# Seven products of zeros ahead of the first attention scores of a three-block mixer kernel

## The chip, the cores and the metric

The kernel runs on one core of a Trainium2 chip, in one launch. The metric is the device time in microseconds (us) of that core, as a median over runs. Engines are called as the profile calls them: PE is TensorE's matrix product and PEld its weight load, DVE is VectorE, ACT is ScalarE, POOL is GpSimd, SP is SyncE, from whose queue all DMAs of this kernel are issued.

## The reference

Three blocks follow each other on two batches of 448 tokens and 768 channels: causal attention with 12 heads of 64, a mixer over tokens and channels, and a gated mixer. Only the first touches this change.

```python
def _attn_ref(q, k, v):                      # (2, 12, 448, 64) each
    scores = scale * np.matmul(q, k.transpose(0, 1, 3, 2))
    scores = np.where(mask, -1000000000.0, scores)
    scores = scores - np.max(scores, axis=-1, keepdims=True)
    attn = np.exp(scores)
    attn = attn / (np.sum(attn, axis=-1, keepdims=True) + 1e-09)
    return np.matmul(attn, v).astype(np.float32)

def _moe_ref(x, w_tok1, w_tok2, w_ch1, w_ch2):
    h = np.maximum(x.transpose(0, 2, 1) @ w_tok1, 0.0) @ w_tok2
    u = x + h.transpose(0, 2, 1)
    return (u + np.maximum(u @ w_ch1, 0.0) @ w_ch2).astype(np.float32)
```

The weights arrive as 64-bit floats; the kernel decodes them to 32 bits on chip (`decode`, L134 to L138) and splits them in two parts.

## The kernel before

**Attention.** The heads are taken two at a time: 12 pairs (b, n), six for each batch. For a pair, `prep_qk` loads k (L325) and the two halves of q (L327), and `load_v` loads v (L333). `probabilities` makes the scores of one half of the query rows of one head: PE multiplies q and k (L371, float32, moving widths of 64, 448, 128, 320 columns) into the tile `s_ps`, of which there are two buffers; DVE reads `s_ps`, adds the mask and takes the row extremes (L376, into `pe` and `mx`); ACT makes a bias of `mx` (L383) and the exponential (L385), then the 16-bit upper part (`hl`, L397); POOL, or DVE for a few, makes the lower part (L398); a transposing DMA on SP's queue turns both (`pT`, L401). A few of the 48 go through PE for the transposition instead (`t_ps`, L391). `values` multiplies `pT` with the two parts of v (`x_ps`, L424 to L426). The two parts of v, `vh` and `vl`, come from `prep_v`: a maximum of v on DVE (`am`, L340), a small product on PE that spreads it (`vm`, L342), `vh` on ACT (L347), `vl` on DVE (L348).

**Around it.** While attention runs, the token weights are decoded (ACT L134, DVE L137 and L138, POOL L145 and L108), the mixer over tokens runs for two pairs at a time (`a_ps`, `u_ps`), and the first products of the channel mixer (`r_ps`) are used to fill. From about 140 us on PE runs channel products and the gated block.

**What sets the order.** The program is written in one order, but a scheduler places the instructions of each engine: it keeps its own estimate of when operands are ready and gives a tile's instructions priorities (`high_priority` with negative offsets for the fill). Afterwards every engine works strictly through its own list, and so does SP's queue with the DMAs. An instruction that is added at the start can therefore change the lists behind it.

**The start.** The first pair's k and q are the first DMAs. Until they land PE has nothing to do. DVE sets q's unused quarters and parts of `vh` to zero meanwhile (L305 to L312), and POOL builds `ident` and `mask`.

Of the kernel before, what the change touches and what calls it, by code (L numbers as in the profile page):

```python
# [9 lines left out]
BF16 = mybir.dt.bfloat16  # L10
F16 = mybir.dt.float16
F32 = mybir.dt.float32
# [16 lines left out]
def mixer_kernel(  # L29
# [18 lines left out]
    nc = tc.nc  # L48
# [5 lines left out]
    P = 128  # L54
# [21 lines left out]
    const = ctx.enter_context(tc.tile_pool(name="const", bufs=1))  # L76
# [4 lines left out]
    rsum = sc.tile([P, B, NFF], F32, name="rsum")  # L81
    rs = ExitStack()
    rpool = rs.enter_context(tc.tile_pool(name="rpool", bufs=1))

    ident = const.tile([P, P], F32, name="ident")
    make_identity(nc, ident)
# [191 lines left out]
    with ExitStack() as at:  # L278
# [8 lines left out]
        ps_a = at.enter_context(tc.tile_pool(name="ps_a", bufs=1, space=PSUM))  # L287
        ps_u = at.enter_context(tc.tile_pool(name="ps_u", bufs=2, space=PSUM))
        ps_e = at.enter_context(tc.tile_pool(name="ps_e", bufs=2, space=PSUM))

        w1h = tokw.tile([P, NQ, T], F32R, name="w1h")
        w1l = tokw.tile([P, NQ, T], F32R, name="w1l")
# [666 lines left out]
```

## Time and profile before

| | |
|---|---|
| median of 3 runs | 405.92 us (405.43 to 406.95) |
| the profiled execution | 404.83 us, of which 403.0 us are the span from the first to the last instruction |
| PE busy | 387.5 us (96% of the span) |
| DVE, ACT, POOL busy | 296.7, 249.9, 188.8 us |
| the stretch of attention and token mixer | about 5 to 140 us |

A busy engine in the profile may be slow as well as full: a product's record lasts as long as the product takes at whatever clock it gets. The lists of the engines are given below as "order" listings; they tell what stands where, and nothing of times. A number behind a name there is the buffer's, and it differs between the two kernels by ten or so.

### The profile page before, as it was taken

What the parts mean: (1) busy time and instruction counts of PE and PEld (TensorE: products, weight loads), DVE (VectorE), ACT (ScalarE), POOL (GpSimd) and SP (SyncE); (2) the same over time, 40 slices, a digit from 0 to 9 for tenths busy, and PEclk for the clock granted to TensorE, in tenths of its full rate; (3) what the DMA queues carried; (4) which work ended last, traced back from release to release, by engine and by line L of the source; (5) the groups of instructions that cost most, each with busy time, mean ns of one, the idle gap of its engine ahead of it and who ended that gap; (6) DMA issues with size and microseconds to landing.
All of it is one profiled execution on the core that took longest, in us unless ns stands there. A gap on an engine that the chain in (4) does not pass through costs nothing.

```text
span 403.0 us, 7341 instructions
## 1 busy us (share of the span) xinstructions
PE 387.5 (96%) x2638; PEld 267.2 (66%) x2638; DVE 296.7 (74%) x709; ACT 249.9 (62%) x479; POOL 188.8 (47%) x195
## 2 busy tenths in 40 slices
PE   5988999989999999999999999999999999999996
PEld 3555777778887999999887555555554445555554
DVE  5988999767986825544367978778698998599742
ACT  3988778766977555755789793634275275655100
POOL 3865863684888464443352174254112158325200
PEclk9999999999999999999999999999999999999999
DMA  7999998999889835575640505545502322100122
GB/s 215 235 226 227 258 183 211 171 195 268 213 189 227 233 129 176 184 245 204 230 158 0 157 1 141 173 130 181 183 8 85 104 87 71 54 0 0 70 105 101
DMA packets 57524, 60.74 MB, mean 151 GB/s; under 512 B 43664, under 2 KB 49040, under 8 KB 57488
## 3 DMA queue, kind: packets, MB, share of 16 engines
q1 hardware_dynamic: 57488, 60.28, 57.0%
q8 instruction: 21, 0.34, 0.3%
q14 instruction: 15, 0.12, 0.1%
HBM read 47.29 MB, written 2.75 MB: 124 GB/s over the span
## 4 chain that ended last, share of the span: by engine, by line
PE 73%; DVE 12%; DMA 7%; ACT 3%; issue 2%; SPq 1%; POOL 1%; DVEq 0%; ACTq 0%; POOLq 0%
PE y_ps L214 7%; PE y_ps L212 7%; PE y_ps L213 7%; PE r_ps L212 6%; PE r_ps L214 6%; PE r_ps L213 6%; DMA vr<-in 3%; DVE pe L376 3%; PE o_ps L212 2%; PE o_ps L214 2%; PE ug_ps L213 2%; PE ug_ps L214 2%; PE o_ps L213 2%; PE ug_ps L212 2%; PE v_ps L213 2%; PE v_ps L212 2%
## 5 line engine op out<-in xcount | busy, mean ns | idle before, releaser
L371 PE MATMUL s_ps<-k,q 128*128 128x64 f32 (+3 forms) x216 | 54.8, 393 | 5.3 <-DMA q<-in 4.6
L108 POOL TENSOR_TENSOR wlo<-wm,whi 128x768 fp32r<-128x768 f32 x20 | 42.9, 2147 | 35.5 <-ACT whi L147 31.8
L212 PE MATMUL r_ps<-uh,whi 128*128 128x448 f32 x144 | 54.7, 380 | 0.0
L213 PE MATMUL r_ps<-ul,whi 128*128 128x448 f32 x144 | 52.9, 367 | 0.0
L214 PE MATMUL r_ps<-uh,wlo 128*128 128x448 f32 x144 | 52.9, 367 | 0.0
L398 POOL TENSOR_TENSOR hl<-pe,hl 128x512 f16<-128x512 f32 x34 | 42.2, 1245 | 18.3 <-ACT hl L397 14.9
L212 PE MATMUL y_ps<-r,w 128*128 128x448 f16 x144 | 50.6, 353 | 0.0
L213 PE MATMUL y_ps<-r,w 128*128 128x448 f16 x144 | 50.6, 352 | 0.0
L214 PE MATMUL y_ps<-r,w 128*128 128x448 f16 x144 | 50.4, 352 | 0.0
L134 ACT ACTIVATE wm<-wraw 128x768 f32<-128x768 f32 (+2 forms) x34 | 27.3, 804 | 34.5 <-DMA wraw<-in 27.3
L137 DVE TENSOR_SCALAR wm<-wm 128x768 int32<-128x768 int32 (+2 forms) x34 | 22.7, 668 | 29.6 <-ACT wm L134 29.6
L371 PEld LDWEIGHTS s_ps<-k,q 128*128 128x128 f32 x216 | 30.8, 200 | 12.8 <-DVE vh L310 4.6
L376 DVE CUSTOM_DVE_ANT_0 pe<-s_ps,mask 128x192 f32<-128x192 f32 (+3 forms) x84 | 34.5, 442 | 3.0 <-PE s_ps L371 2.8
L138 DVE SCALAR_TENSOR_TENSOR wm<-wraw,wm 128x768 int32<-128x768 int32 (+2 forms) x34 | 33.1, 973 | 0.7
L273 POOL TENSOR_TENSOR y<-yt,ul 128x448 f32<-128x448 f32 x10 | 13.2, 1322 | 42.7 <-DVE yt L271 42.7
L385 ACT ACTIVATE pe<-pe,bias 128x448 f32<-128x448 f32 (+3 forms) x67 | 32.2, 526 | 0.3
L424 PE MATMUL x_ps<-vh,pT 128*128 128x65 f16 (+1 forms) x240 | 25.6, 197 | 4.1 <-DMA pT<-hl 2.8
L212 PEld LDWEIGHTS r_ps<-uh,whi 128*128 128x128 f32 x144 | 27.1, 188 | 2.9 <-issue 0.4
L213 PEld LDWEIGHTS r_ps<-ul,whi 128*128 128x128 f32 x144 | 27.1, 188 | 2.9 <-issue 0.4
L424 PEld LDWEIGHTS <-pT 128*128 128x128 f16 (+1 forms) x240 | 21.2, 98 | 11.7 <-issue 5.3
L214 PEld LDWEIGHTS r_ps<-uh,wlo 128*128 128x128 f32 x144 | 27.0, 188 | 2.5
L206 POOL TENSOR_TENSOR w<-w2m,w 128x768 f16<-128x768 f32 x12 | 20.5, 1727 | 15.7 <-ACT w2m L205 12.8
(219 smaller groups left out, 1038.4 us busy)
## 6 DMA issues: line engine op xcount, KB each, us to landing
wraw<-in SPq DMA_DIRECT2D x36, 768.0 KB, 4.4
wraw<-in SPq DMA_DIRECT2D x14, 512.0 KB, 3.9
vr<-in SPq DMA_DIRECT2D x12, 320.0 KB, 4.3
k<-in SPq DMA_DIRECT2D x12, 224.0 KB, 3.7
q<-in SPq DMA_DIRECT2D x24, 112.0 KB, 3.8
out<-ob SPq DMA_DIRECT2D x11, 224.0 KB, 1.9
wraw<-in SPq DMA_DIRECT2D x3, 256.0 KB, 4.4
sgr<-in SPq DMA_DIRECT2D x3, 224.0 KB, 2.8
```

Source lines behind the costliest of these rows:

```text
L108: nc.gpsimd.tensor_sub(lo, src, f32(hi))
L134: nc.scalar.activation(m, words.bitcast(F32)[:, :, 1], AF.Prelu, scale=2.0 ** -112, alpha=-(2.0 ** 32))
L137: nc.vector.tensor_scalar(mi, mi, 3, None, ALU.logical_shift_left)
L138: nc.vector.scalar_tensor_tensor(mi, words[:, :, 0], 29, mi, ALU.logical_shift_right, ALU.bitwise_or)
L212: nc.tensor.matmul(ps, lh, rh, start=i == 0 and not begun, stop=False)
L213: nc.tensor.matmul(ps, lh, rl, start=False, stop=False)
L214: done.append(nc.tensor.matmul(ps, ll, rh, start=False, stop=ended and i == n - 1).ins)
L371: last_s[0] = nc.tensor.matmul(ps[:, o:o + m], qp[:, q0:q0 + P], k2[:, ks], start=True, stop=True).ins
L376: last_mx[0] = nc.vector.tensor_tensor_reduce(out=pe[:, cs], in0=ps[:, cs], in1=mask0 if i == 0 else mask[:, MASKS[i]], scale=-1.0 / math. ...
L385: nc.scalar.activation(pe[:, cs], pe[:, cs], AF.Exp, bias=bias[:, j:j + 1], scale=-1.0)
L398: ins = (nc.vector if lo_dve else nc.gpsimd).tensor_sub(hl[:, 1], pe, hl[:, 0]).ins
L424: nc.tensor.matmul(o, ph, vh[:, c, h, :D + 1], start=j == 0, stop=False)
```

## The change

A tile `warm` of 128x512 bfloat16 zeros is made by DVE, and seven products of it with itself, 128x512 each, are issued on PE into a PSUM tile that the token mixer uses later. Nothing reads them.

```diff
@@ -82,6 +82,9 @@
     rpool = rs.enter_context(tc.tile_pool(name="rpool", bufs=1))
 
+    warm = const.tile([P, 512], BF16, name="warm")
+    nc.vector.memset(warm, 0.0)
+
     ident = const.tile([P, P], F32, name="ident")
@@ -287,6 +290,10 @@
         ps_e = at.enter_context(tc.tile_pool(name="ps_e", bufs=2, space=PSUM))
+
+        pw = ps_a.tile([P, 512], F32, tag="a", name="warm_ps")
+        for _ in range(7):
+            nc.tensor.matmul(pw, warm[:, :P], warm, start=True, stop=True)
 
         w1h = tokw.tile([P, NQ, T], F32R, name="w1h")
```

Lines from L86 on move down by 3, and from L291 on by 7. The lists of all engines change with it. On PE, before: the nine products of the first pair's scores open the list.

```order
L371 MATMUL s_ps_207<-k2_182,q0_163 128x64
L371 MATMUL s_ps_207<-k2_182,q0_163 128x448
L371 MATMUL s_ps_229<-k2_182,q0_163 128x128
L371 MATMUL s_ps_229<-k2_182,q0_163 128x64
L371 MATMUL s_ps_229<-k2_182,q0_163 128x320
L371 MATMUL s_ps_295<-k2_182,q0_163 128x448
L371 MATMUL s_ps_306<-k2_182,q0_163 128x128
L371 MATMUL s_ps_306<-k2_182,q0_163 128x64
L371 MATMUL s_ps_306<-k2_182,q0_163 128x320
```

After, on PE, the end of the seven products and the scores behind them:

```order
L296 LDWEIGHTS warm_74
L296 MATMUL warm_ps_153<-warm_74 128x512
L378 MATMUL s_ps_217<-k2_192,q0_173 128x64
L378 MATMUL s_ps_217<-k2_192,q0_173 128x448
L378 MATMUL s_ps_239<-k2_192,q0_173 128x128
```

The first two rows stand seven times ahead of the scores, each product with a weight load of its own; the scores follow in the order they had. PE's two lists hold the same instructions from there on, in another order in places, up to the first `r_ps`, which starts at 79.8 us in the trace of before, and are nearly the same behind it.

On ACT, before, from the exponentials of the first `s_ps` on (`wraw` is a raw token weight):

```order
L385 ACTIVATE pe_208<-pe_208,bias_214 128x448
L397 CAST hl_219<-pe_208 128x512
L134 ACTIVATE wm_246<-wraw_195 128x256
L383 ACTIVATE bias_237<-mx_231 128x2
L385 ACTIVATE pe_230<-pe_230,bias_237 128x192
L385 ACTIVATE pe_230<-pe_230,bias_237 128x320
L383 ACTIVATE bias_298<-mx0_157 128x2
```

After, the same place on ACT:

```order
L392 ACTIVATE pe_218<-pe_218,bias_224 128x448
L390 ACTIVATE bias_247<-mx_241 128x2
L404 CAST hl_229<-pe_218 128x512
L392 ACTIVATE pe_240<-pe_240,bias_247 128x192
L392 ACTIVATE pe_240<-pe_240,bias_247 128x320
L137 ACTIVATE wm_256<-wraw_205 128x256
L390 ACTIVATE bias_308<-mx0_167 128x2
```

The second decode (`wraw_195`, now `wraw_205`) moved behind two exponentials, and the bias ahead of the cast. A third decode, `wm_380`, which stood 11 rows further down, moved some 40 rows down, with its DVE and POOL instructions; its DMA moved 20 rows down on SP.

On DVE, before, from the second `vl` on (each 128x1 `mx` row belongs to the row above it; `am_370` is the maximum of the third pair's v, `vr_368`):

```order
L348 SCALAR_TENSOR_TENSOR vl1_181<-vr_197,sv_327,vh1_177 128x640
L376 ISA pe_659,mx_660<-s_ps_658,mask_87 128x192
L376 ISA mx_660 128x1
L376 ISA pe_659,mx_660<-s_ps_658,mask_87 128x320
L376 ISA mx_660 128x1
L376 ISA pe0_155,mx0_157<-s_ps_691,mask_87 128x448
L376 ISA mx0_157 128x1
L340 TENSOR_REDUCE am_370<-vr_368 128x1
```

After, the same place on DVE:

```order
L355 SCALAR_TENSOR_TENSOR vl1_191<-vr_207,sv_337,vh1_187 128x640
L347 TENSOR_REDUCE am_380<-vr_378 128x1
L383 ISA pe_669,mx_670<-s_ps_668,mask_89 128x192
L383 ISA mx_670 128x1
L383 ISA pe_669,mx_670<-s_ps_668,mask_89 128x320
L383 ISA mx_670 128x1
L383 ISA pe0_165,mx0_167<-s_ps_701,mask_89 128x448
L383 ISA mx0_167 128x1
```

The maximum of v moved ahead of three reads of scores. On SP the load of that v, which stood behind four transposing DMAs, stands behind three.

## Rows read from the trace of the kernel before

**Rows 1.** Stretches: busy us and instructions of each engine, granted clock, DMA share, GB/s.
```profile
core 0: us, PE busy (x) PEld busy (x) DVE busy (x) ACT busy (x) POOL busy (x), PEclk, DMA share, GB/s
4.60:11.40 6.80, 6.80 (x21) 4.46 (x21) 3.91 (x19) 4.45 (x10) 2.25 (x3) 1.00 0.96 291
11.40:24.00 12.60, 10.33 (x97) 6.47 (x97) 11.16 (x41) 12.50 (x32) 9.66 (x10) 1.00 1.12 219
24.00:80.00 56.00, 52.38 (x589) 40.84 (x588) 50.10 (x161) 43.83 (x102) 34.43 (x45) 1.00 1.01 214
80.00:140.00 60.00, 58.06 (x550) 50.13 (x549) 47.22 (x110) 45.79 (x99) 44.04 (x48) 1.00 0.99 219
140.00:390.00 250.00, 250.00 (x1332) 159.28 (x1329) 177.59 (x364) 143.29 (x238) 96.32 (x77) 1.00 0.36 116
```

**Rows 2.** Groups by shape, PE from 4.5 to 10 us: busy us, mean ns.
```profile
L371 PE MATMUL s_ps<-k,q 128*128 128x448 f32 x4 | 3.5, 981 | 0.0
...
L371 PE MATMUL s_ps<-k,q 128*128 128x64 f32 x4 | 1.2, 401 | 4.6 <-DMA q<-in 4.6
```

**Rows 3.** The same, PE from 28 to 40 us.
```profile
L371 PE MATMUL s_ps<-k,q 128*128 128x448 f32 x8 | 3.9, 575 | 0.0
...
L371 PE MATMUL s_ps<-k,q 128*128 128x64 f32 x10 | 1.7, 257 | 0.0
```

**Rows 4.** Timeline, PE: start, us, instructions; two records make a product.
```profile
4.60 6.79 PE L371 MATMUL s_ps<-k,q 128*128 128x64 f32 x18 [4.60 <-DMA q<-in]
...
31.32 2.13 PE L371 MATMUL s_ps<-k,q 128*128 128x64 f32 x10
...
259.98 0.35 PE L214 MATMUL y_ps<-r,w 128*128 128x448 f16 x1
260.17 0.35 PE L212 MATMUL y_ps<-r,w 128*128 128x448 f16 x1
```

**Rows 5.** Instructions that write or read `vm` (L342): min, median, max ns.
```profile
L342 PEld LDWEIGHTS <-am x4: 96/97/98, 11.0 to 28.9; 128*128 128x128 bf16 x4
```

**Rows 6.** Timeline, DVE.
```profile
0.87 0.43 DVE L305 MEMSET q<- 64x448 f32 x1 [0.87 <-PEq L944]
1.44 0.43 DVE L306 MEMSET q<- 64x448 f32 x1
...
7.03 0.22 DVE L376 CUSTOM_DVE_ANT_0 pe<-s_ps,mask 128x64 f32<-128x64 f32 x1 [1.98 <-PE s_ps L371]
...
20.93 0.36 DVE L376 CUSTOM_DVE_ANT_0 pe<-s_ps,mask 128x192 f32<-128x192 f32 x1
...
21.62 0.62 DVE L376 CUSTOM_DVE_ANT_0 pe<-s_ps,mask 128x448 f32<-128x448 f32 x1
...
23.66 0.69 DVE L340 TENSOR_REDUCE am<-vr 128x1 bf16<-128x512 f32 x1 [1.41 <-DMA vr<-in]
```

**Rows 7.** Timeline, ACT.
```profile
7.84 0.20 ACT L383 ACTIVATE bias<-mx 128x2 f32<-128x2 f32 x1 [0.28 <-DVE mx L376]
8.08 0.91 ACT L385 ACTIVATE pe<-pe,bias 128x64 f32<-128x64 f32 x2
9.01 0.62 ACT L397 CAST hl<-pe 128x512 f16<-128x512 f32 x1
10.36 0.44 ACT L134 ACTIVATE wm<-wraw 128x256 f32<-128x256 f32 x1 [0.73 <-DMA wraw<-in]
...
14.43 0.43 ACT L134 ACTIVATE wm<-wraw 128x256 f32<-128x256 f32 x1
```

**Rows 8.** Timeline, SP's queue: start and us of the issue.
```profile
13.79 2.75 SPq L401 DMA_TRANSPOSE pT<-hl  x2
...
17.93 1.40 SPq L401 DMA_TRANSPOSE pT<-hl  x1
19.43 0.53 SPq L333 DMA_DIRECT2D vr<-in  x1
```

**Rows 9.** Waits of PE from 11 to 80 us, then of DVE from 5 to 80 us: total, times, longest.
```profile
PE x_ps L424 <- DMA pT<-hl: 2.8, 3, 1.4
...
DVE am L340 <- DMA vr<-in: 4.2, 3, 1.8
```

## The prediction

> **What bounds the kernel now.** I read the stretches first. From 140 to 390 us PE is busy in 250.00 of 250.00 us [rows 1]: whatever time PE wins or loses before it gets there moves the end by the same amount, since no wait is left in it that could swallow a gain. So the change is worth what it does to the moment at which PE is through with attention. Ahead of 140 us the reader should look at how much room there is: PE is busy throughout 4.60 to 11.40 us (6.80 of 6.80), then it idles 2.27 us up to 24 us, 3.62 us from there to 80 us and 1.94 us up to 140 us [rows 1]. In 11.40 to 24 us it is not PE but ACT that is full, 12.50 of 12.60 us, with DVE at 11.16; from 24 to 80 us PE (52.38 of 56.00) and DVE (50.10) stand close together [rows 1].
>
> Second, the shapes. The granted clock reads 1.00 in every stretch, but the durations of the first products contradict it: the same 448-column product takes 981 ns up to 10 us and 575 ns from 28 us on, the 64-column one 401 against 257 ns [rows 2, 3]. The difference for 448 columns is 406 ns, for 64 columns 144 ns, so it is 262 ns for 384 columns more; what grows with the columns takes 1.51 ns a column (580/384) at first and 0.83 ns (318/384) later, close to a factor of two. I take it that the first products ran at the lower level (1.2 GHz), after an idle PE, and the later ones at the upper one (2.4 GHz), and that the clock column simply holds no record of the start. Third, the lists of the engines, since the change moves instructions; fourth, what ACT, DVE and SP do there [rows 6 to 8].
>
> **The seven products and their tile.** DVE's first instruction starts at 0.87 us, and a memset of 448 words takes 0.43 us, with 0.57 us from one start to the next [rows 6]. The new one, 256 words of the same width, takes about 0.25 us, so PE can begin at about 1.3 us. No bfloat16 product of 512 columns is in the trace; the nearest is the 16-bit one of 448 columns, which follows its predecessor by 0.19 us at the upper level [rows 4]. That gives 0.22 us for 512 columns, or 0.43 us at the lower level: seven take 1.5 to 3.0 us. A weight load of 128 columns in bfloat16 takes 97 ns [rows 5]; if none of the seven hides behind a product, add 0.7 us. They end between 2.8 and 5.0 us, most likely at 4.3 us, at the lower level with the loads hidden. The first scores start at 4.60 us, because q lands then [rows 4]; PE's idle start is the cover, and the cost is nothing, at worst 0.4 us. On DVE the memset pushes the zeros of q and what follows by 0.25 to 0.57 us; the 1.98 us that DVE idles until 7.03 us hide it [rows 6]. Without that cover it would cost just that much. q's DMAs don't queue behind it.
>
> **What the clock gives.** The nine score products of the first pair have 1984 columns and take 6.79 us in 18 records; five of a later pair, 1024 columns, take 2.13 us at the upper level [rows 4]. At that rate 1984 columns take 4.13 us, so 2.66 us is the most that the clock can return on PE. How long the lower level lasted follows from the same two: what it cost, 2.66 us, is 0.45 of its length at the ratio of 1.51 to 0.83 ns a column, and half of it at a ratio of two, so 5.3 to 5.9 us; I take 5.7 us, since everything up to 10 us is long [rows 2] and PE began at 4.60 us. If the seven products start the same delay at 1.3 us, the rise comes at about 7.0 us, 2.4 us into the scores: the loss shrinks to 2.4/5.7 of it, and 1.5 us are returned. Bounds: 0 (the zeros or the small gap behind them do not carry over) and 2.66 us (full from the first score). I take 1.5 us, as the row is the only delay that this trace shows.
>
> The Trainium skill, "TensorE: Matmul & The Clock Gate", Part 1, speaks against taking one delay over: it says that the moment of the rise is not tied to the kernel's start, and that the same kernel gets a different number of slow products from run to run. One profiled execution can't show that. By it the sum would lie anywhere between the two bounds just named, and it would be no truer at 1.5 us than at 2 us.
>
> **How much of that arrives.** From 11.40 to 24 us ACT is full, so PE's 1.5 us arrive only as far as ACT gets ahead. ACT loses two waits there in the first 11 us: 0.28 us for the first `mx` and 0.73 us for a raw token weight [rows 7]. The new list has that decode two exponentials later, when its weight has landed (it landed at 10.36 us), and the next bias ahead of the cast; so the 0.73 us become a wait for the second product's `mx`, which is shorter the faster that product ran. Of the 1.01 us I count half, 0.5 us, because the first product, which DVE begins to read at 7.03 us [rows 6], would still run at the lower level by the delay taken above, and only the second one gains. The third decode, 0.43 us on ACT at 14.43 us [rows 7], leaves the full stretch and is paid back after 24 us, where ACT has 12 us of room (43.83 of 56.00) [rows 1]. Sum on ACT at 24 us: 0.9 us, with bounds of 0.43 and 1.44 us. ACT's 0.9 us are less than PE's 1.5, so they count.
>
> **What the new order gives or takes.** Behind that, the lists differ up to about the first `r_ps`. PE does the same work, so only its idle time can change: 2.27 + 3.62 = 5.89 us from 11.40 to 80 us [rows 1], of which 2.8 us are waits for transposed probabilities [rows 9]. I see no row that says that the new order has more or less of it, and put it at nothing; the bounds are the rivals below. The sum is -0.9 us. Against the profiled execution, 404.83 us (403.0 us of span), that makes 403.9 us; the median of the runs stands 1.09 us above that execution, so the forecast is 405.0 us. A difference of 0.5%, 2 us, is about what a measurement of this kernel can tell from no change; this lies inside it.
>
> **Rival: slower, DVE is blocked on v.** DVE works in order, and its waits for v's loads already cost 4.2 us in three places [rows 9]. In the largest early one, before, DVE had read three scores (20.93 to 22.24 us) and then waited 1.41 us [rows 6]. Now the maximum of v stands ahead of those reads. The load was issued at 19.43 us and landed 4.2 us later, at about 23.6 us. In the new list three, not four, transposing DMAs stand ahead of it, so it can go out from 16.5 us (13.79 + 2.75) [rows 8], or, if the buffer of v comes free late, as before: it lands between 20.7 and 23.6 us. Then the maximum (0.69 us) and the three reads (1.31 us) end between 22.7 and 25.6 us, where the reads ended at 22.24 us: exponentials, transposes and values of that pair come 0.5 to 3.4 us later, though v's own chain comes earlier. It decides from a landing at about 21.2 us on, where the delay passes the 0.9 us won. With the worst of it, 3.4 - 0.9 = 2.5 us slower: 408.4 us; in the middle, 2.0 - 0.9 = 1.1 us slower: 407.0 us. Against it: one transposing DMA less ahead of the load, and a decode less on DVE ahead of the maximum.
>
> **Rival: faster, everything arrives.** The clock is up with the first score and ACT and DVE take the scores as they come: -2.66 us, 403.3 us. If the new order also removes the 2.8 us of PE's waits for transposes [rows 9], 400.5 us. For it: DVE waits 1.98 us for the first score and would take it earlier [rows 6]. Against it: ACT, full to 24 us.
>
> **Rival: the clock doesn't rise earlier.** Then only the order acts: the third decode's 0.43 us leave ACT's full stretch, and the time is 405.5 us, in the same class as the forecast.
>
> **How the numbers follow.** The forecast (gain of some 0.4 to 1.5 us, the order neutral) 0.38; no earlier rise 0.12; faster with clock and order together 0.31; slower by DVE's block 0.19, half of it past 2 us, though other waits of this kind in the moved part (the lists differ for 60 us) can take its place, so I leave nearly all of it on the slower side. That is faster 0.31, same 0.51, slower 0.18. The range leaves out the outer half of the faster rival and of the slower one: from 401.9 us (half way from 403.3 to 400.5) to 407.7 us (half way from 407.0 to 408.4).
>
> **What would show it.** In the trace after: seven products from about 1.3 to 4.3 us and the first score still at about 4.6 us (right on cover); the 448-column product of the first score shorter than 981 ns, the first one of 575 ns before 7.5 us (right on the clock); the nine products done by 9.7 us instead of 11.4; ACT without the 0.73 us wait; the first `r_ps` about 0.9 us before 79.8 us, and the same gain at the end. It is wrong if the first score starts after 5 us, if its products still take 981 ns up to 10 us, if DVE's waits for v grow past 4.2 us, or if PE's idle time from 11.4 to 80 us differs from 5.9 us by more than 2 us: then the order, not the clock, made the result.

## The result, and the profile after

The changed kernel takes 410.18 us (408.00 to 412.31, median of 8 runs), the kernel before 405.89 us in the same comparison: a ratio of 1.0101, with a 95% interval of 1.0069 to 1.0132. It is slower by 4.3 us, where 405.0 us were forecast and 407.7 us was the end of the range. The profiled execution of the changed kernel is its quickest, 408.0 us, of which 406.2 us are the span: 3.2 us more than before.

Stretches of the kernel after, with the columns of [rows 1]:

```profile
core 0: us, PE busy (x) PEld busy (x) DVE busy (x) ACT busy (x) POOL busy (x), PEclk, DMA share, GB/s
4.60:11.40 6.80, 6.32 (x20) 3.98 (x21) 4.12 (x22) 4.47 (x10) 0.78 (x1) 1.00 0.92 287
11.40:24.00 12.60, 11.34 (x103) 7.32 (x104) 11.56 (x46) 11.54 (x30) 10.14 (x11) 1.00 0.96 196
24.00:80.00 56.00, 49.40 (x565) 38.22 (x563) 47.04 (x150) 43.89 (x100) 35.86 (x48) 1.00 0.90 202
80.00:140.00 60.00, 57.61 (x527) 49.34 (x524) 46.62 (x112) 46.06 (x100) 42.54 (x44) 1.00 0.99 225
140.00:390.00 250.00, 250.00 (x1356) 160.45 (x1355) 180.10 (x368) 144.83 (x242) 97.25 (x79) 1.00 0.35 117
```

Against [rows 1], PE's idle time is 0.48 us more up to 11.4 us, 1.0 us less from there to 24 us (1.26 for 2.27), 3.0 us more up to 80 us (6.60 for 3.62) and 0.45 us more up to 140 us: 2.9 of the 3.2 us in all. From 140 to 390 us both run without a gap. So the start did gain, by half a microsecond, and the stretch from 24 to 80 us lost six times as much.

The start, on PE (start, us, instructions):

```profile
1.17 3.17 PE L296 MATMUL warm_ps<-warm 128*128 128x512 bf16 x7 [1.17 <-DVE warm L86]
4.77 4.88 PE L378 MATMUL s_ps<-k,q 128*128 128x64 f32 x12 [0.44 <-DMA q<-in]
9.87 1.22 PE L378 MATMUL s_ps<-k,q 128*128 128x128 f32 x6 [0.21 <-DVE mx L383]
10.93 0.22 PE L349 MATMUL vm<-ident_b,am 128*128 128x128 bf16 x1
```

The same scores by shape, PE from 4.5 to 10 us (busy us, mean ns), to be held against [rows 2]:

```profile
L378 PE MATMUL s_ps<-k,q 128*128 128x448 f32 x4 | 2.7, 774 | 0.0
...
L378 PE MATMUL s_ps<-k,q 128*128 128x64 f32 x4 | 1.2, 400 | 0.4 <-DMA q<-in 0.4
```

The products end at 4.34 us, ahead of the scores; the 64-column product is as slow as before (400 for 401 ns), the 448-column one quicker on average (774 for 981 ns). That fits a clock that rises in the middle: the first clock record of the trace, which is the rise, stands at 8.7 us, before at 10.4 us.

And waits of PE from 11 to 80 us and of DVE from 5 to 80 us (total, times, longest), to be held against [rows 9]:

```profile
PE x_ps L431 <- DMA pT<-hl: 3.8, 6, 1.0
PE s_ps L378 <- DVE mx L383: 1.6, 5, 0.4
PE u_ps L498 <- DVE al L488: 1.2, 1, 1.2
```

```profile
DVE pe L383 <- PE s_ps L378: 5.7, 6, 1.8
DVE am L347 <- DMA vr<-in: 4.4, 5, 2.1
```

PE's waits are more and shorter than before: six for transposed probabilities instead of three. None of them is the 3 us by itself. The first `r_ps`, which stood at 79.81 us, comes late, in spite of the gain at the start:

```profile
82.03 0.45 PE L215 MATMUL r_ps<-uh,whi 128*128 128x448 f32 x1
```

### The profile page after: what moved, and what is told of

Its sections match the earlier page's. It is cut to its first block, busy times and chain, and to the rows that moved or that the text cites. A ratio compares the mean times of both kernels' runs of the same rounds, so it can differ in the third digit from the quotient of the medians.

```text
span 406.2 us, 7349 instructions
## 1 busy us (share of the span) xinstructions
PE 390.9 (96%) x2645; PEld 267.9 (66%) x2645; DVE 296.9 (73%) x710; ACT 250.8 (62%) x479; POOL 188.7 (46%) x195
## 4 chain that ended last, share of the span: by engine, by line
PE 73%; DVE 10%; DMA 9%; issue 3%; ACT 2%; SPq 1%; POOL 1%; DVEq 0%; ACTq 0%; POOLq 0%
PE y_ps L215 7%; PE y_ps L216 7%; PE y_ps L217 7%; PE r_ps L215 7%; PE r_ps L216 7%; PE r_ps L217 7%; DMA vr<-in 6%; PE s_ps L378 3%; DVE pe L383 3%; PE o_ps L217 2%; PE o_ps L215 2%; PE o_ps L216 2%; PE ug_ps L216 2%; PE ug_ps L217 2%; PE ug_ps L215 2%
## 5 line engine op out<-in xcount | busy, mean ns | idle before, releaser
L378 PE MATMUL s_ps<-k,q 128*128 128x64 f32 (+3 forms) x216 | 53.8, 389 | 3.3 <-DVE mx L383 2.2
L140 DVE TENSOR_SCALAR wm<-wm 128x768 int32<-128x768 int32 (+2 forms) x34 | 21.7, 638 | 33.3 <-ACT wm L137 33.3
L141 DVE SCALAR_TENSOR_TENSOR wm<-wraw,wm 128x768 int32<-128x768 int32 (+2 forms) x34 | 35.0, 1028 | 0.6
```

The lines of the kernel that those rows point to most:

```text
L140: nc.vector.tensor_scalar(mi, mi, 3, None, ALU.logical_shift_left)
L141: nc.vector.scalar_tensor_tensor(mi, words[:, :, 0], 29, mi, ALU.logical_shift_right, ALU.bitwise_or)
L378: last_s[0] = nc.tensor.matmul(ps[:, o:o + m], qp[:, q0:q0 + P], k2[:, ks], start=True, stop=True).ins
```

## Experiment 1: products and lists apart

The change does two things: it adds products, and it moves the lists. To take them apart, the lists were written down from both kernels and put back with ordering edges between an engine's neighbours, edges that carry no semaphore:

```diff
         mixer_kernel(tc, *args)
+        in_this_order(nc, tc)
```

`w7_old` has the seven products with the lists of before, `w0_new` no products with the lists of after. `w5_old` has five products (with five, the scheduler leaves the lists alone), `w12_old` twelve with the lists of before.

```diff
-        for _ in range(7):
+        for _ in range(12):
```

> The seven products of zeros, with every engine's list in the order of the kernel before (pinned by issue-order edges). Theory A, the moved lists cost the 4.3 us: with the old lists the kernel is back at 405.9 us or a little below it, 404.4 to 406.2 us, since the clock rises some 1.7 us earlier (8.7 us in the trace after, 10.4 us in the trace before). Theory B, the products themselves cost it (they start PE early, the clock falls again or rises at another time, and later stretches run at the lower level): 409 to 411 us, and a mean granted clock below 1.0 in most executions. A mixture (3 us from the lists, 1 to 2 us from the clock) would show as 406.5 to 408 us.

> No products and no tile of zeros; every engine's list in the order of the kernel after. Theory A: the loss stays, 408.5 to 411 us. Theory B: 405 to 406.5 us. If the products give a gain of their own, this one is slower than the kernel after by that gain, 0.5 to 1.5 us.

> Five products in place of seven, nothing pinned: the scheduler then leaves every list as before. Theory A: 404.4 to 406.2 us. Theory B, if the loss is in the products: about five sevenths of it, 408 to 409.5 us. The five end at about 3.3 us, 1.3 us before the first scores; if the early start counts for the clock all the same, it rises before 10.4 us.

> Twelve products with the old lists: 12 x 0.43 us from 1.2 us on end at 6.3 us at the lower level, so the first score starts 1.7 us late, but with no idle PE in front of it. Theory A with a gain from the clock: the clock rises before the first or second score, PE makes up what it started late, 405 to 406.5 us. If PE's early time is not what bounds the kernel there but the chain of DVE and ACT behind the first score, the late start shows in full: 407 to 407.6 us.

Measured, as ratios to the kernel before (406.59 us) with 95% intervals; a ratio is not simply the quotient of the two medians:

| kernel | median us | ratio |
|---|---|---|
| `w7_old` | 405.46 | 0.9976 (0.9954 to 0.9998) |
| `w0_new` | 410.18 | 1.0086 (1.0059 to 1.0113) |
| `w5_old` | 406.33 | 1.0002 (0.9985 to 1.0019) |
| `w12_old` | 407.28 | 1.0023 (0.9997 to 1.0048) |

Without a single product, the moved lists alone take the time of the changed kernel, within the intervals (1.0086 against 1.0101). With the lists held, none of the three numbers of products moves the ratio by more than 0.25%; twelve land where the late start was expected to show (407 to 407.6 us), but the interval still includes no change. The ordering edges are not what costs, since `w7_old` has them as well. The loss is the lists'.

The shapes tell how far the products did their work. The 448-column scores from 4.5 to 10 us, in `w7_old`:

```profile
L378 PE MATMUL s_ps<-k,q 128*128 128x448 f32 x4 | 2.0, 579 | 0.0
```

and in `w0_new`, which has none:

```profile
L371 PE MATMUL s_ps<-k,q 128*128 128x448 f32 x4 | 3.0, 836 | 0.0
```

In `w7_old` all of them run at the upper level (575 ns in [rows 3]); in the changed kernel, with the same seven products, part of them. In `w0_new` without products they are nearly as quick as after (836 against 774 ns), in `wnewold` of experiment 3, also without products, just as quick (773 ns), and before they are slow throughout (981 ns). So the moment of the rise differs between executions by as much as seven products move it. In the profiled execution of `w7_old` PE's products got most of the 2.66 us of the prediction's bound: nine take 4.5 us where before they took 6.79. But PE then waits for DVE, and the nine end only 0.7 us earlier, at 10.7 us:

```profile
4.62 3.23 PE L378 MATMUL s_ps<-k,q 128*128 128x64 f32 x12 [0.37 <-DVE vh L317]
9.50 1.22 PE L378 MATMUL s_ps<-k,q 128*128 128x128 f32 x6 [1.66 <-DVE mx L383]
```

The stretches of the same execution:

```profile
4.60:11.40 6.80, 5.12 (x22) 3.17 (x23) 4.67 (x23) 4.43 (x10) 2.25 (x3) 0.96 0.98 282
11.40:24.00 12.60, 10.01 (x78) 5.86 (x77) 10.62 (x40) 11.97 (x32) 9.51 (x10) 0.89 1.18 216
```

PE idles 1.68 and 2.59 us here where before it idled 0 and 2.27, and the granted clock, 0.89 in the second stretch, has gone back to the lower level for part of it. This execution is the slowest of the twelve of `w7_old` (408.03 us); nine of them have a mean clock of 1.0 and take 404.85 to 407.01 us. So it shows one way in which a gain at the start can be lost, not what the median run does.

## Experiment 2: one place in the lists?

The trace of after has one place that looks like the loss. DVE, from 47 to 53 us:

```profile
47.33 0.68 DVE L141 SCALAR_TENSOR_TENSOR wm<-wraw,wm 128x512 int32<-128x512 int32 x1
49.24 0.36 DVE L383 CUSTOM_DVE_ANT_0 pe<-s_ps,mask 128x192 f32<-128x192 f32 x1 [1.23 <-PE s_ps L378]
...
52.15 0.69 DVE L347 TENSOR_REDUCE am<-vr 128x1 bf16<-128x512 f32 x1 [2.13 <-DMA vr<-in]
```

SP's queue around the load that DVE waits for:

```profile
40.83 0.33 SPq L123 DMA_DIRECT2D wraw<-in  x1
41.27 1.25 SPq L408 DMA_TRANSPOSE pT<-hl  x1
42.63 0.96 SPq L123 DMA_DIRECT2D wraw<-in  x1
43.70 4.10 SPq L408 DMA_TRANSPOSE pT<-hl  x2
47.86 0.57 SPq L340 DMA_DIRECT2D vr<-in  x1
```

The load goes out at 47.86 us behind five others, though v's buffer was free from 39.6 us on, when the last reader (`vl`, 1.77 us from 37.85 us) ended; before, its counterpart went out at 37.20 us. DVE stands 2.13 us. A second candidate is the third slab of the first weight matrix, whose decoding has moved from 14 us to the 36 to 41 us in which DVE is full. `v_first` has the lists of after with the load alone moved up:

```diff
 L327 DMA q_164<-in 64x448 x2
+L333 DMA vr<-in 128x640
 L120 DMA wraw<-in 128x512
 L401 DMA_TRANSPOSE pT<-hl 128x8x128
 L120 DMA wraw<-in 128x512
-L401 DMA_TRANSPOSE pT<-hl 128x8x128 x2
-L333 DMA vr<-in 128x640
-L401 DMA_TRANSPOSE pT<-hl 128x8x128
+L401 DMA_TRANSPOSE pT<-hl 128x8x128 x3
```

`w_early` has the slab where it was, on SP, ACT, DVE and POOL; on ACT:

```diff
 L385 ACTIVATE pe<-pe,bias 128x320
+L134 ACTIVATE wm<-wraw 128x256
 L383 ACTIVATE bias<-mx 128x2
...
 L393 ACTIVATE pT<-t_ps 128x512
-L134 ACTIVATE wm<-wraw 128x256
 L347 ACTIVATE vh_177<-vr,sv 128x10x64
```

`vw` has both edits, and `c_oldnew` the lists of before up to about 37 us and those of after behind that.

```diff
-PE, DVE, ACT, POOL, SP: entries of after from 0 on
+PE, DVE, ACT, POOL, SP: entries of before up to 257, 85, 59, 41, 34, of after from there on
```

> No products, every list as in the changed kernel but one entry: the load of v that VectorE waits for at 50 us stands six places earlier in SP's list, right behind the two q loads that precede it there by 8 us. Theory V (that late load is the loss of 50 to 53 us): VectorE's wait of 2.1 us goes, and 1.5 to 2.1 us of the 3.5 us that the new lists cost come back, 408.1 to 408.7 us, ratio 1.004 to 1.005. Rival (VectorE is ahead of TensorE there, its wait on scores 1.2 us just before says so, and the wait only changes its name): under 0.5 us, 409.7 us or more.

> No products, every list as in the changed kernel but for the third slab of the first weight matrix: its load, ScalarE's conversion, VectorE's two decoding steps and GpSimd's two splits stand where the kernel before has them, at 13 to 16 us, not at 31 to 41 us. Theory W (the decoding, 0.4 + 1.2 us on VectorE at 36 to 41 us, holds up the masks that TensorE waits for there): 1.2 to 1.6 us come back, 408.6 to 409.0 us, ratio 1.005 to 1.006. Theory V: the loss sits later, so at most 0.5 us, 409.7 us or more.

> Both edits of the two kernels beside it at once, no products. If two separate places make the loss, their gains add: 2.7 to 3.5 us come back, 406.7 to 407.5 us, ratio 1.000 to 1.002. If one place hides the other, it is no better than the better of the two, 408.1 us or more.

> No products; the lists of the kernel before up to about 37 us (the first 257 of TensorE's entries, 85 of VectorE's, 59 of ScalarE's, 41 of GpSimd's, 34 of SP's hold the same instructions in both versions), those of the changed kernel from there on, the late load of v included. Theory V (the loss is made behind the cut): 409 to 410 us, ratio 1.006 to 1.009. Theory W (it is made ahead of the cut, by the slab's late decoding): 406.3 to 407.3 us, ratio 0.999 to 1.002.

| kernel | median us (before: 406.39) | ratio |
|---|---|---|
| `v_first` | 408.15 | 1.0058 (1.0029 to 1.0088) |
| `w_early` | 409.54 | 1.0081 (1.0051 to 1.0110) |
| `vw` | 409.40 | 1.0089 (1.0056 to 1.0121) |
| `c_oldnew` | 408.40 | 1.0055 (1.0028 to 1.0082) |

DVE's wait for v is gone in `v_first`, and the wait for scores ahead of it has stayed:

```profile
49.05 0.36 DVE L376 CUSTOM_DVE_ANT_0 pe<-s_ps,mask 128x192 f32<-128x192 f32 x1 [1.27 <-PE s_ps L371]
...
49.74 0.68 DVE L340 TENSOR_REDUCE am<-vr 128x1 bf16<-128x512 f32 x1
```

The median of `v_first` is 2 us lower than that of `w0_new`, its ratio lower by 0.0028 with intervals that overlap: the load may be worth 1 to 2 us here, and not all of the loss. (The execution profiled is the quickest of its twelve, 405.98 us.) The slab is worth nothing that shows. The two edits together are no better than the lists they started from: `vw` differs from `w_early` by the same load, and there moving it returned nothing (1.0089 for 1.0081). `c_oldnew` lies between what both theories gave: by the medians about half of the loss comes with the later lists.

## Experiment 3: the halves again, and the load in three settings

`on_v` is `c_oldnew` with the load moved up; `wnewold` has the lists of after first (with the slab as before, since the later lists need it) and those of before from the same cut on; `w7_v` is the changed kernel with the load moved up, products and all.

```diff
 L327 DMA q_163<-in 64x448 x2
+L333 DMA vr<-in 128x640
 L325 DMA k_1110<-in 128x448
...
-L333 DMA vr<-in 128x640
```

```diff
-PE, DVE, ACT, POOL, SP: entries of after from 0 on
+PE, DVE, ACT, POOL, SP: entries of after up to 257, 85, 59, 41, 34, of before from there on
```

> No products; the lists of the kernel before up to about 37 us and those of the changed kernel behind it, as in the run that took 408.4 us (ratio 1.0055), but with the late load of v moved six to nine places up in SP's list, to where the kernel before issues it. Theory V (that one load makes most of the loss behind 37 us): 1.5 to 2.0 us come back, 406.4 to 406.9 us, ratio 1.000 to 1.002. Rival S (the loss is many small waits of TensorE, none of which is this load's): under 0.5 us, 407.9 us or more, ratio 1.004 or more.

> No products; the other half: the changed kernel's lists up to about 37 us, but with the third slab of the first weight matrix where the kernel before has it (the lists behind need it there), and the lists of the kernel before from 37 us on. If the loss lies behind the cut alone: 406.2 to 406.9 us, ratio 0.999 to 1.002. If the lists ahead of the cut also cost (the kernels that carry them had their clock recorded at the half level about twice as often as those that don't): 407.2 to 408.4 us, ratio 1.002 to 1.005.

> The changed kernel itself, seven products and its lists, with that one load of v six places earlier in SP's list. Theory V: 1.5 to 2 us of the changed kernel's 410.2 come back, and the products, worth 0.9 us with the lists held, may show: 407.3 to 408.7 us, ratio 1.002 to 1.006. Rival S: 409.5 us or more, ratio 1.007 or more.

| kernel | median us (before: 405.95) | ratio |
|---|---|---|
| `on_v` | 408.17 | 1.0049 (1.0014 to 1.0083) |
| `wnewold` | 412.13 | 1.0145 (1.0101 to 1.0188) |
| `w7_v` | 408.39 | 1.0067 (1.0032 to 1.0102) |

In `on_v` the edit did what it should and returned nothing (408.40 to 408.17). Waits of DVE from 37 to 80 us, in `c_oldnew`:

```profile
DVE am L340 <- DMA vr<-in: 3.6, 3, 2.8
DVE sv L344 <- PE vm L342: 2.2, 1, 2.2
DVE rd L452 <- PE x_ps L426: 1.5, 1, 1.5
```

and in `on_v`:

```profile
DVE sv L344 <- PE vm L342: 2.6, 1, 2.6
DVE rd L452 <- PE x_ps L426: 1.9, 2, 1.5
...
DVE am L340 <- DMA vr<-in: 1.2, 2, 0.7
```

The wait for v shrank by 2.4 us, but the two waits for PE grew by 0.8 us, and PE's idle time from 24 to 80 us stayed (5.78 and 5.59 us). That fits a DVE that was ahead of PE there, as far as one execution of each can tell. In `w7_v` the same edit returned 1.8 us by the medians (410.18 to 408.39; in the ratios 0.0034, with intervals that overlap), as it had returned 2.0 in `v_first`. So in the lists of after that load may be a third to a half of the loss, and with other lists ahead of it (`on_v`, `vw`) it returns nothing that shows. And `wnewold` was a surprise: the earlier lists of after, with the slab moved back, followed by the later ones of before have a higher ratio than either whole. A half of a list is good or bad together with the other half, so "which place is it" has no single answer in these runs. The theory of one place had fallen as the whole answer, and what was left to try was that the lists of before are good as a whole.

## Experiment 4: other lists from the same scheduler

If the lists of after are bad in some way of their own, other lists should fall on either side of before. If those of before are unusually good, all others should be slower. Six, eight, nine and ten products each make the scheduler write different lists, which differ from those of before and of after in hundreds of rows. The edit is the count alone:

```diff
-        for _ in range(7):
+        for _ in range(6):
```

> Six products, and the planner's own lists for that, which differ from those of the kernel before and from those of seven products. Theory N (one place in the lists of seven products is bad): the lists of six have another such place or none, so the time may fall on either side of before, 404.5 to 408 us, ratio 0.997 to 1.005. Theory L (the lists of the kernel before are an unusually good draw, and any other that the planner makes costs about 1%): 408.5 to 411.5 us, ratio 1.006 to 1.014.

> Eight products with the planner's own lists, again different from all others. Theory L: 408.5 to 411.5 us, ratio 1.006 to 1.014. Theory N: on either side of before, 404.5 to 408 us, ratio 0.997 to 1.005.

> Nine products with the planner's own lists, again different. Theory L: 408.5 to 411.5 us, ratio 1.006 to 1.014. Theory N: on either side of before, 404.5 to 408 us, ratio 0.997 to 1.005.

> Ten products with the planner's own lists, again different. Theory L: 408.5 to 411.5 us, ratio 1.006 to 1.014. Theory N: on either side of before, 404.5 to 408 us, ratio 0.997 to 1.005.

| products, own lists | median us (before: 406.19) | ratio |
|---|---|---|
| 6 | 413.27 | 1.0161 (1.0110 to 1.0211) |
| 8 | 412.76 | 1.0152 (1.0104 to 1.0199) |
| 9 | 411.97 | 1.0130 (1.0088 to 1.0171) |
| 10 | 421.01 | 1.0362 (1.0321 to 1.0403) |

(The planner in the expectations is the scheduler.) All are slower, by more than was expected, and one by 15 us; of the five sets of lists that were tried with their products, those of seven cost least. Where each loses differs. PE's idle time in the profile of eight products sits from 80 to 140 us (7.6 us), in that of ten also behind 140 us (6.1 us), where before there is none:

```profile
80.00:140.00 60.00, 52.42 (x490) 44.17 (x490) 43.06 (x113) 42.37 (x91) 41.52 (x44) 1.00 0.87 213
```

```profile
140.00:200.00 60.00, 53.88 (x321) 48.19 (x322) 27.60 (x43) 30.35 (x60) 22.82 (x19) 0.91 0.52 154
```

The first fence is of eight products, the second of ten. So in this kernel other lists from the same scheduler cost 1.0 to 3.6%, and those of eight and of ten do not lose in the same place. (The products themselves vary too, but with the lists held five, seven and twelve were worth no more than 0.25%.) What the lists of before have that all these lack is not shown. Nor are the five independent draws. In their traces all five put the load of v ahead of the fourth transposing DMA, and all five hold the third slab's load back: it goes out at 9.39 us before, at 15.52 us with ten products and at 28.9 us or later with the others. The slab alone returned nothing in `w_early`, but a cause that the early rows of all five share is not excluded, and the ratio of `wnewold` would fit one. Lists that differ from before for a reason other than these products were not tried.

## Why the prediction was wrong

**Cover, right.** The products run from 1.17 to 4.34 us (about 1.3 to 4.3 forecast), and the first score starts at 4.77 us for 4.60, released by q's DMA.

**Clock, right in kind, not in its worth.** The rise came earlier, but at 8.7 us and not at 7.0; the nine scores were done at about 11.1 us rather than 9.7, and ACT's wait of 0.73 us became one of 0.60 us for `mx`. ACT's busy time from 11.4 to 24 us fell from 12.50 to 11.54 us, about the 0.9 us of the sum, of which the third decode that moved away is 0.43. With the lists held, seven products gave a ratio of 0.9976, about 1 us. That is close to the 0.9 us of the sum, but the agreement proves little: with the lists of after they gave nothing (410.18 us with and without), and five and twelve gave nothing either. So the term is between 0 and 1 us, and these runs don't tell more. The Trainium skill, "TensorE: Matmul & The Clock Gate", Part 1, says that the moment of the rise is not tied to the kernel's start and that one kernel gets a different number of slow products from run to run. The shapes agree, over different kernels with the same nine scores: the 448-column mean is 773 to 981 ns in the eight without products, and 774, 579 and 758 ns in the three with seven. In those three the products start alike, at 1.17 us, and the rise is recorded at 8.7, 4.0 and 6.3 us. One profiled execution of before could not carry a delay of 5.7 us.

**Order, the step that failed.** "I see no row that says that the new order has more or less of it, and put it at nothing." It cost 3.6 us in `w0_new` (410.18 against 406.59 us), four times the term that the sum rested on. The lack of a row was read as zero, with chances on both sides; yet the lists differ for 60 us on five engines, and each of the five other sets that the scheduler wrote here lost, 0.9 to 3.6%. The prediction's own signs came close to naming it: PE's idle time from 11.4 to 80 us went from 5.89 to 7.86 us, and the first `r_ps` came 2.2 us late where 0.9 us early was forecast. The same step held that PE does the same work, so that only its idle time can change; that left out a clock that falls back later (the mean granted clock is below 0.999 in 12 of the 14 runs with the lists of after).

**Rival "slower", right in direction, not in its place.** DVE's wait for the third v, on which it was priced, was harmless: the load went out at 17.32 us and DVE waited 0.43 us for it, where before it waited 1.41. DVE's waits for v's loads as a whole are 4.4 us, as they were 4.2: by the letter a sign of being wrong, but 0.2 us explain nothing. That another wait of this kind can take its place, as the prediction added, holds in part: it is the load of experiment 2.

```profile
20.54 0.69 DVE L347 TENSOR_REDUCE am<-vr 128x1 bf16<-128x512 f32 x1 [0.43 <-DMA vr<-in]
```

**Open.** How the 4.3 us divide is not settled to the last. In runs with a mean granted clock of 0.999 or more the lists of after take 407.7 and 408.0 us (two runs, of `w0_new` and of the changed kernel), the kernel before 405.8 us (mean of 49 runs): so about 2 us are lost at full clock. The other 12 of these 14 runs have a lower mean clock, against 47 of 96 runs of before, and take 408.2 to 412.3 us. At an equal clock, 0.995 to 0.996, eight of them average 410.0 us and 40 runs of before 406.9 us, 3.1 us apart. So the larger part of the loss is there at an equal clock, and the lower clock adds the smaller part. Why these lists lose is open beyond the waits shown. `w7_old` has the lowest median, but its interval (0.9954 to 0.9998) all but reaches no change.

## What to carry to other kernels

An edit that a scheduler sees changes more than its own instructions: compare the lists first, and don't price a changed list at zero. Here five new sets out of five were worse; whether other kernels share that is not shown. Hold the lists and measure the edit alone; here that turned 1% slower into no loss. And before a wait in a trace is called the loss, ask who would be late next: moving the load that ends a 2 us wait of DVE returned 1 to 2 us by the medians with one set of lists and nothing with another, where DVE then waited longer for PE.

## What the hardware showed that was not expected

TensorE's clock need not stay up once it has risen. In the profile of `c_oldnew`, in the middle of attention, the granted clock falls to the lower level of 1.2 GHz for part of two stretches. Stretches of 3 us, with the columns of [rows 1]:

```profile
48.00:51.00 3.00, 2.42 (x23) 1.68 (x22) 1.91 (x6) 3.00 (x8) 1.69 (x2) 1.00 1.24 248
51.00:54.00 3.00, 1.84 (x21) 1.32 (x22) 1.19 (x2) 1.85 (x5) 1.31 (x2) 0.88 1.22 196
54.00:57.00 3.00, 3.00 (x12) 2.62 (x11) 3.00 (x9) 1.28 (x3) 1.21 (x3) 0.55 1.06 239
57.00:60.00 3.00, 2.99 (x17) 2.08 (x17) 3.00 (x12) 2.39 (x7) 1.86 (x2) 1.00 0.70 133
```

PE had waited 1.74 us for transposed probabilities just before (its product starts at 52.16 us), and then works without a gap through a stretch of granted clock 0.55. If the gap is what let the clock fall, a gap on PE is paid twice, once as idle time and once in slow products behind it; `w7_old` has the same sequence, waits of 1.66 and 2.00 us (ending at 9.50 and 23.89 us), each with a fall of the clock soon behind it. But `w12_old` waits 1.9 us once, for the token mixer, and keeps a granted clock of 1.00 up to 390 us, so such a gap alone does not decide it. Lists with more gaps show more of it: the mean granted clock over all runs is 0.998 before, 0.995 in the 14 runs with the lists of after and 0.981 in those of ten products. That links the two; no run changed the gaps alone, so it is not shown that the gaps make the clock fall, nor that the falls make the rest of the loss.
